# Centring each token ahead of its transposes instead of folding the mean into the first layer's weights, with a new order table, in a gated linear-attention and MLP kernel on Trainium2

## The chip, the cores and the metric

The kernel runs on one core of one Trainium2 chip. The metric is the time on the device in microseconds, from the start to the end of one execution; lower is better. The core has five engines that run their own queues in order: PE (matrix products and transposes, into PSUM), DVE (VectorE), ACT (ScalarE), POOL (GpSimd) and SP, which here only issues DMAs.

## The reference

The program first runs a gated linear recurrence for every batch (4) and head (8), over 768 steps with 48 channels, then puts the heads side by side (8 x 48 = 384) and runs a layer norm and a two-layer MLP on each token:

```python
mag = np.sqrt(a_re * a_re + a_im * a_im)
scale = np.minimum(mag, 0.999) / (mag + 1e-06)
a_re_n, a_im_n = (a_re * scale, a_im * scale)
for t in range(S):
    new_re = ar * S_re - ai * S_im
    new_im = ar * S_im + ai * S_re
    S_re, S_im = (new_re + k_t v_t^T, new_im)      # 48 x 48 for each batch and head
    y[t] = q_t @ S_re
x = y as (batch, 768, 384)
mu = mean(x); var = mean((x - mu) ** 2)
xn = (x - mu) / np.sqrt(var + 1e-06) * g_ln
out = x + np.maximum(xn @ w_ch1, 0.0) @ w_ch2      # w_ch1: 384 x 1536, w_ch2: 1536 x 384
```

The matrix products run in bf16 with sums in fp32.

## The kernel before

The recurrence is computed in chunks of 128 steps. Two chunks of one batch make a pair; there are 12 pairs P (three for each batch) and 24 chunks n = 2P + c. "Token" below means such a chunk of 128 tokens. Pair 0 has its first stage in two parts (heads 0 to 3 and 4 to 7; `PARTS`), so its steps have names such as `ks.0.1.0`.

For each pair the steps are, by their names in the table:

- loads by SP: `are`, `aim` (the gate), `k`, `q`, `vf` (k, q, v of one chunk each, 192 KB). POOL issues the loads of the two weight matrices (`wl.0` to `wl.5`), which are cast to bf16 on the way.
- decay and phase: `ln`, `iv`, `u`, `th` on ACT, `r`, `r2`, `l`, `lc` on DVE, POOL or ACT; `dec` and `ph` are sums over the steps as matmuls; `e`, `en`, `sin`, `cos` on ACT. For a pair in `QUARTER` the cosine comes from a quarter turn that two more matmuls (`qt`) add to the phase; otherwise from `abs` on ACT or DVE.
- `ke`, `qe`, `ks`, `qs`: k and q times decay and trigonometric factors, on DVE or POOL. Their transposes: `kT`, `qT` on PE followed by a copy `ksT`, `qsT` out of PSUM, or a DMA transpose issued by SP under the same name `ksT`, `qsT`.
- per chunk n: `am` (scores), `atm` (mask), `gm` and `G` (state passed on; `dps`, `decc` give its decay), `v` (cast of v), `y` (output of the recurrence, in PSUM), `x` (its copy to SBUF in bf16).
- the MLP: `bn` (mean and variance of x, on DVE), `xtr` and `xT` (x transposed on PE, copied out of PSUM), `mm1.P.g.part` (first layer, both tokens of the pair, six matmuls each), `relu`, `mm2.n.part` (second layer, four matmuls each), `rstd`, and the output: `ot` on DVE (scale by rstd and add x in one instruction from PSUM) or `oa` on ACT and `ot` on POOL; `st` stores.

The layer norm is folded: the factor 1/sqrt(var) is applied to the output of the second layer (`oa` or `ot`). The mean is taken off through the weights: `wgc` (three DVE instructions, L380) makes the matrix gc = g_ln / 384, `wp` (L389, nine matmuls of 512 columns) gives the column means of g_ln * w_ch1 in PSUM, and `wc` (L393, nine DVE instructions of 128x512) replaces w1b, the bf16 copy of w_ch1, by g_ln * w_ch1 less that mean. So x is transposed as it is, `xtr` needs `x` alone, and `bn` is wanted by `rstd` only. The first `mm1` needs all `wc` of its third of the columns.

At the start PE runs 113 filler matmuls (`warm`, L776) between the real ones.

The order is written out by hand: `PLAN` is one list of `name:engine` with the PSUM bank behind the engine's letter (P, A, V, G for POOL, S). Each engine gets its steps in the order of the list, and nothing is moved later. A step may carry `@other`: it then also waits until `other` has finished (used on POOL, "turns at the shared port"). `RINGS` gives the number of buffers of each tile; `x` has 10.

Of the kernel before, what the change touches and what calls it, by code (L numbers as in the profile page):

```python
# [56 lines left out]
ph.0.1:P1 l.2.0:V qe.0.1.0:V qe.0.0.0:V sin.0.1:A1 ph.0.0:P0 q.1.1:S k.1.0:S lc.2.0:V dps.0:P6 car.0.1:V1
dec.2.0:P2 pad.ks.1:G vf.0.0:S vf.0.1:S car.0.0:A0 qs.0.1.1:V sin.0.0:A0 qt.0.1:P1 qs.0.0.1:V qe.1.0.1:V
decc.0:V6 qt.0.0:P0 th.2.0:A aim.3.0:S cos.0.1:A1 ks.0.1.1:V ks.0.0.1:V cos.0.0:A0 ph.1.0:P4 sin.1.0:A4 k.1.1:S
tab.log.2:A ln.3.0:A ks.0.1.0:V qs.0.1.0:V en.2.0:A2 qs.0.0.0:V warm.103:P1 warm.104:P1 warm.105:P1 warm.106:P1  # L60
warm.107:P1 warm.108:P1 qT.0:P6 pad.qs.1:G ks.0.0.0:V car.1.0:V4 wl.2:G qT.1:P0 iv.3.0:A wp.1:P1 qsT.0:V6
qsT.1:V0 kT.0:P6 qs.1.0.1:G@ks.0.0.0 wc.1.1:V1 qt.1.0:P4 wc.1.0:V1 ksT.0:A6 wp.0:P0 e.2.0:A2 aim.4.0:S wc.1.2:V1
kT.1:P7 am.0:P2 tab.trig.3:A cos.1.0:A4 v.0:A wc.0.0:V0 wc.0.1:V0 wc.0.2:V0 ph.2.0:P0 ksT.1:V7 am.1:P6
ke.1.0.0:G@wc.0.2 wp.2:P4 atm.0:V2 sin.2.0:A0 gm.0:P5 G.0:A5 are.4.0:S y.0:P2 x.0:A2 qt.2.0:P0 r.3.0:G gm.1:P5
atm.1:V6 cos.2.0:A0 ke.1.0.1:V y.1:P3 x.1:A3 qs.1.0.0:V vf.1.1:S xtr.0:P2 ks.1.0.1:V vf.1.0:S ks.1.0.0:V
warm.109:P6 warm.110:P6 warm.111:P6 warm.112:P6 qT.2:P6 xT.0:A2 qT.3:P0 xtr.1:P1 qsT.2:V6 kT.3:P2 xT.1:V1
r2.3.0:G@ks.1.0.0 kT.2:P3 ksT.3:V2 mm1.0.0.0:P6 ksT.2:V3 th.3.0:A v.1:G qsT.3:A0 am.3:P0 tab.log.4:A ln.4.0:A
G.1:V5 wl.3:G mm1.0.0.1:P6 mm1.0.1.1:P2 atm.3:V0 mm1.0.1.0:P2 am.2:P0 relu.0.0:A6 q.2.1:S wc.2.2:V4 relu.0.1:A2
gm.2:P5 G.2:A5 wl.4:G wl.5:G u.3.0:A k.2.0:S ph.3.0:P6 y.3:P2 wc.2.0:V4 qe.2.0.1:G@wc.2.0 atm.2:V0 y.2:P3 x.3:A2
q.3.1:S x.2:A3 gm.3:P5 wc.2.1:V4 iv.4.0:A mm1.0.2.0:P0 xtr.2:P4 pad.ks.2:G k.2.1:S xtr.3:P3 xT.2:A4  # L70
ke.2.0.0:G@wc.2.1 abs.3.0:V6 car.3.0:V6 xT.3:V3 G.3:V5 bn.2:V mm1.0.2.1:P0 q.2.0:S tab.trig.5:A sin.3.0:A6
bn.1:V bn.3:V mm1.1.0.1:P2 mm1.1.1.1:P4 mm1.1.1.0:P4 ke.2.0.1:G cos.3.0:A mm1.1.0.0:P2 mm2.1.0:P6 mm2.0.0:P7
vf.2.0:S relu.1.1:A4 relu.1.0:A2 mm1.1.2.1:P4 are.6.0:S mm2.1.1:P6 relu.0.2:V0 r.4.0:G r2.4.0:G th.4.0:A bn.0:V
qe.2.0.0:G l.3.0:V mm2.0.1:P7 mm2.2.0:P2 tab.log.6:A u.4.0:A lc.3.0:V q.3.0:S are.5.0:S qs.2.0.0:V dec.3.0:P0
rstd.0:G e.3.0:A0 ks.2.0.1:V mm2.2.1:P2 qs.2.0.1:V en.3.0:A0 mm1.1.2.0:P4 ks.2.0.0:V mm2.1.2:P6 l.4.0:V lc.4.0:V
dps.3:P3 qe.3.0.0:G@lc.4.0 qT.4:P0 rstd.1:A qT.5:P1 relu.1.2:V4 vf.2.1:S mm2.2.2:P2 k.3.0:S dec.4.0:P4
qe.3.0.1:G ln.6.0:A oa.1:A6 qsT.4:V0 kT.4:P0 mm2.0.2:P7 qs.3.0.0:V qs.3.0.1:V k.3.1:S iv.6.0:A decc.3:V3
ln.5.0:A qT.6:P6 ksT.4:V0 mm2.3.0:P0 e.4.0:A4 dps.4:P3 v.2:G@qs.3.0.1 en.4.0:A4 ot.2:V2 ot.0:V7 ke.3.0.1:G
gm.4:P2 qsT.5:A1 ksT.5:S am.4:P4 aim.5.0:S qsT.6:V6 mm2.3.1:P0 G.4:A2 decc.4:V3 qT.7:P1 iv.5.0:A ph.4.0:P2
atm.4:V4 tab.trig.7:A sin.4.0:A2 aim.6.0:S am.5:P6 ke.3.0.0:G ks.3.0.1:G ks.3.0.0:V qsT.7:V1 k.4.1:S abs.4.0:A2  # L80
vf.3.1:S vf.3.0:S kT.6:P5 kT.7:P1 y.4:P4 q.5.0:S car.4.0:A2 r.5.0:G@ks.3.0.0 x.4:A4 r.6.0:G v.3:G mm2.3.2:P0
ot.1:G th.5.0:A atm.5:V6 y.5:P2 vf.4.0:S ksT.6:V5 xtr.4:P3 am.6:P4 vf.4.1:S k.4.0:S ksT.7:V1 am.7:P6 xT.4:V3
q.4.1:S q.4.0:S x.5:A2 xtr.5:P1 cos.4.0:A ph.5.0:P2 xT.5:A1 k.5.0:S atm.6:V4 ot.3:V0 q.5.1:S st.3:S gm.6:P1
mm1.2.1.1:P4 atm.7:V6 y.6:P0 mm1.2.1.0:P4 th.6.0:A G.6:A1 sin.5.0:A2 r2.6.0:G y.7:P6 x.6:V0 abs.5.0:A2
relu.2.1:V4 x.7:A6 gm.7:P1 xtr.6:P0 mm1.2.2.0:P2 G.7:V1 ke.4.0.1:G xtr.7:P6 xT.6:V0 r2.5.0:G mm1.2.0.1:P4
xT.7:V6 bn.6:V cos.5.0:A mm1.2.0.0:P4 ke.4.0.0:G relu.2.0:V4 st.1:S mm1.3.0.0:P6 qe.4.0.1:G tab.log.8:A u.5.0:A
u.6.0:A mm1.3.0.1:P6 mm1.2.2.1:P2 mm1.3.1.0:P4 l.5.0:V qe.4.0.0:V lc.5.0:V qs.4.0.1:V relu.3.0:A6 ks.4.0.0:V
aim.7.0:S ks.4.0.1:V mm1.3.1.1:P4 qs.4.0.0:V are.7.0:S dec.5.0:P6 mm1.3.2.0:P0 relu.2.2:A2 relu.3.1:A4 e.5.0:A6
l.6.0:V mm2.4.0:P2 are.8.0:S qT.8:P5 lc.6.0:V en.5.0:A6 aim.8.0:S ln.7.0:A iv.7.0:A bn.7:V ke.5.0.0:G@lc.6.0
mm2.5.0:P4 dec.6.0:P6 qsT.8:V5 qe.5.0.0:G kT.9:P3 bn.5:V k.5.1:S v.4:A r.7.0:G mm1.3.2.1:P0 relu.3.2:V0 ln.8.0:A  # L90
bn.4:V en.6.0:A6 ksT.8:S iv.8.0:A ksT.9:V3 mm2.6.0:P5 qe.5.0.1:G mm2.4.1:P2 mm2.6.1:P5 am.8:P0 mm2.6.2:P5
rstd.3:G mm2.5.1:P4 e.6.0:A6 qsT.9:S am.9:P6 gm.8:P3 rstd.2:A mm2.4.2:P2 r2.7.0:V u.7.0:A st.2:S tab.trig.9:A
th.7.0:A atm.8:V0 ph.6.0:P0 atm.9:V6 q.6.0:S y.8:P6 st.0:S sin.6.0:A0 ke.5.0.1:G@r2.7.0 G.8:V3 qs.5.0.0:G
vf.6.1:S y.9:P7 x.9:A7 ot.4:V2 mm2.7.0:P2 mm2.5.2:P4 are.9.0:S ks.5.0.0:V x.8:V6 ks.5.0.1:V qs.5.0.1:V
qe.6.0.0:V bn.8:V gm.9:P3 xtr.9:P7 car.6.0:A0 abs.6.0:A0 oa.5:A4 cos.6.0:A xT.9:V7 r.8.0:G@qe.6.0.0 mm2.7.1:P2
ph.7.0:P0 bn.9:V q.6.1:S qe.6.0.1:G car.7.0:A0 abs.7.0:A0 xtr.8:P7 xT.8:V7 k.6.0:S mm2.7.2:P2 G.9:V3
mm1.4.1.0:P6 oa.7:A2 sin.7.0:A0 qT.11:P4 mm1.4.1.1:P6 mm1.4.2.1:P2 qs.6.0.0:V vf.5.1:S mm1.4.0.1:P0 l.7.0:V
mm1.4.0.0:P0 relu.4.1:V6 q.7.0:S vf.5.0:S mm1.4.2.0:P2 ke.6.0.0:G@l.7.0 lc.7.0:V qsT.11:A4 qsT.10:S k.6.1:S
qs.6.0.1:V kT.11:P4 ksT.10:S tab.log.10:A ln.9.0:A st.4:S aim.10.0:S vf.6.0:S relu.4.2:A2 aim.9.0:S
ke.6.0.1:G@qs.6.0.1 relu.4.0:V0 dec.7.0:P6 v.5:V ot.6:V5 rstd.4:A ks.6.0.1:V mm2.9.0:P0 iv.9.0:A en.7.0:A6  # L100
# [712 lines left out]
```

## Time and profile before

| | us |
|---|---|
| median of 3 runs | 189.22 (188.66 to 189.74) |
| the profiled execution's own time | 187.9 |
| its span, first to last instruction | 186.1 |
| PE, DVE, ACT, POOL busy | 174.0, 157.7, 158.4, 104.6 |
| first `mm1` starts | 38.1 |
| last `mm2` ends | 182.0 |
| mean granted clock of TensorE | 0.995 of full |

The span is taken by the hardware profiler; the execution's own time has 1.8 us around it. Busy PE includes the filler matmuls (15.6 us by themselves), and matmuls overlap in the pipeline, so that the mean of one in the groups (272 ns for 256 columns) is longer than what it adds in a row (0.655 us for six, or 109 ns each).

### The profile page before, as it was taken

How to read it: one execution, taken by the hardware profiler on the slowest of the kernel's cores; microseconds unless marked ns; L12 is line 12 of the kernel's file. 1: busy time of each engine (PE TensorE's matmuls, PEld its weight loads, DVE VectorE, ACT ScalarE, POOL GpSimd, SP SyncE). 2: the span in 40 equal slices, each digit the busy share in tenths (PEclk: the TensorE clock that was granted, in tenths of full speed). 3: DMA queues.
4: the chain of work that ended last, by engine and by line, in shares of the span. 5: the costliest groups of instructions: out<-in, count | busy, mean ns of one | idle time of the engine just before them, and what ended most of it. 6: DMA issues, size and time to landing. Idle time of an engine off the chain costs nothing.

```text
span 186.1 us, 5096 instructions
## 1 busy us (share of the span) xinstructions
PE 174.0 (94%) x2012; PEld 136.2 (73%) x2012; DVE 157.7 (85%) x281; ACT 158.4 (85%) x226; POOL 104.6 (56%) x126
## 2 busy tenths in 40 slices
...
GB/s 138 281 254 216 188 237 266 171 227 180 213 154 253 221 185 284 210 206 188 206 227 225 182 251 249 212 277 151 201 224 186 210 202 225 153 232 137 36 85 129
DMA packets 132935, 37.55 MB, mean 202 GB/s; under 512 B 127152, under 2 KB 132912, under 8 KB 132912
## 3 DMA queue, kind: packets, MB, share of 16 engines
...
q8 instruction: 15, 0.25, 0.5%
...
## 4 chain that ended last, share of the span: by engine, by line
PE 81%; DVE 6%; DMA 4%; POOL 3%; SPq 2%; issue 1%; ACT 1%; POOLq 0%; DVEq 0%; ACTq 0%
PE banks L726 26%; PE banks L747 25%; PE banks L622 6%; PE banks L599 5%; PE banks L501 4%; PE banks L482 3%; PE banks L672 3%; PE banks L650 2%; PE banks L693 2%; DVE w1b L393 2%; PE banks L675 2%; DMA aim<-in_a_im_dram 2%; DMA k<-in_k_dram 2%; PE banks L497 2%; POOL ke L294 2%
## 5 line engine op out<-in xcount | busy, mean ns | idle before, releaser
L747 PE MATMUL banks<-w2b,h 128*128 128x384 bf16 x288 | 55.9, 326 | 0.0
L726 PE MATMUL banks<-xT,w1b 128*128 128x256 bf16 x432 | 51.8, 272 | 0.0
L726 PEld LDWEIGHTS <-w1b 128*128 128x128 bf16 x432 | 41.3, 98 | 6.6 <-DVE xT L291 0.7
L747 PEld LDWEIGHTS <-h 128*128 128x128 bf16 x288 | 25.7, 97 | 12.3 <-ACT h L737 0.2
L294 POOL TENSOR_TENSOR ke<-k,en 128x384 bf16<-128x384 f32 x19 | 18.4, 976 | 26.8 <-DMA k<-in_k_dram 9.6
L294 DVE TENSOR_TENSOR atm<-banks,mask 128x1024 bf16<-128x1024 f32 x24 | 29.0, 1220 | 2.0 <-PE banks L622 0.6
L781 ACT ACT_TABLE_LOAD x19 | 24.4, 1283 | 1.1 <-PEq L797 0.8
L737 ACT ACTIVATE h<-banks 128x1024 bf16<-128x1024 f32 x22 | 21.8, 1020 | 3.6 <-PE banks L726 3.5
L739 DVE TENSOR_SCALAR h<-banks 128x1024 bf16<-128x1024 f32 x14 | 17.0, 1221 | 4.7 <-PE banks L726 4.6
L759 POOL TENSOR_TENSOR ot<-ot,x 128x384 f32<-128x384 f32 x12 | 10.9, 913 | 16.5 <-ACT ot L752 11.0
L294 POOL TENSOR_TENSOR qe<-q,e 128x384 bf16<-128x384 f32 x16 | 14.5, 917 | 7.0 <-ACT en L486 3.0
L776 PE MATMUL banks<-u_e 128*128 128x256 f16 x113 | 15.6, 299 | 2.2 <-POOL one_b L320 2.2
L294 POOL TENSOR_TENSOR ks<-ke,trig 128x768 bf16<-128x768 bf16 x8 | 13.0, 1642 | 6.0 <-ACT h L737 2.1
L622 PE MATMUL banks<-qsT,ksT 128*128 128x128 bf16 x192 | 14.5, 219 | 1.1 <-ACT e L486 1.1
L776 PEld LDWEIGHTS <-u_e 128*128 128x128 f16 x113 | 12.0, 108 | 4.6 <-POOL u_e L328 1.9
L622 PEld LDWEIGHTS <-ksT 128*128 128x128 bf16 x192 | 12.4, 98 | 3.1 <-issue 0.6
L467 ACT ACTIVATE r<-r,one_b 128x768 f16<-128x768 f16 (+1 forms) x13 | 11.3, 883 | 2.7 <-DVE r L294 2.6
L289 ACT CAST x<-banks 128x384 bf16<-128x384 f32 x18 | 8.4, 481 | 5.8 <-PE banks L675 5.2
L685 DVE BATCH_NORM_STATS2 stats<-x 128x6 f32<-128x384 bf16 x24 | 13.1, 547 | 0.1
L471 DVE SCALAR_TENSOR_TENSOR l<-r,w 128x768 f16<-128x768 f16 (+1 forms) x13 | 11.9, 914 | 1.1 <-ACT r L467 1.0
L294 POOL TENSOR_TENSOR r<-aim,are 128x768 f16<-128x768 f32 x6 | 10.9, 1819 | 3.2 <-DMA q<-in_q_dram 2.6
L453 ACT ACTIVATE w<-are 128x768 f32<-128x768 f32 (+1 forms) x13 | 10.3, 793 | 1.9 <-DMA are<-in_a_re_dram 1.9
...
## 6 DMA issues: line engine op xcount, KB each, us to landing
...
```

The source lines that it names most:

```text
L294: {"DVE": nc.vector, "POOL": nc.gpsimd}[eng(name)].tensor_tensor(**kw)
L467: add(f"u.{X}", lambda S_=S_: act(out=S_("r2"), in_=S_("r2"), func=AF.Ln, bias=one_b), needs=[f"r2.{X}", "one"], uses=[("r2", P)])
L471: nc.vector.scalar_tensor_tensor(out=S_("l"), in0=S_("r2"), scalar=0.5, in1=S_("w"), op0=ALU.mult, op1=ALU.add)
L622: nc.tensor.matmul(ps[:, h], lhsT=T("ksT", n)[:, h], rhs=T("qsT", n)[:, h], start=True, stop=True)
L685: nc.vector.bn_stats(out=T("stats", n), in_=T("x", n))
L726: nc.tensor.matmul(ps[:, jj], lhsT=w1b[:, dc, ts(gi * JG + jj, C)], rhs=T("xT", P)[:, dc].rearrange("p c t -> p (c t)"), start=(dc == 0), ...
L737: act(out=dst, in_=src, func=AF.Relu)
L739: nc.vector.tensor_scalar(out=dst, in0=src, scalar1=0.0, scalar2=None, op0=ALU.max)
L747: nc.tensor.matmul(bank(f"o.{n}")[:, 0:DM], lhsT=T("h", P)[:, j, ts(c, C)], rhs=w2b[:, j], start=(j == 0), stop=(j == NJ - 1))
L759: nc.gpsimd.tensor_tensor(out=T("ot", n), in0=T("ot", n), in1=T("x", n), op=ALU.add)
L776: g.add(f"warm.{i}", lambda i=i: nc.tensor.matmul(bank(f"warm.{i}")[:, 0:256], lhsT=u_e[:, 0, 0], rhs=u_e[:, 1].rearrange("p j t -> p (j t ...
L781: g.add(f"tab.{nm}.{i}", lambda tab=tab: nc.scalar.preload_act_table_set(tab))
```

## The change

Every token is now centred by itself. A new step `xc` (128x384, bf16 in and out, DVE or POOL) subtracts the mean that `bn` has found, a tile ring `xc` of four buffers holds the result, and `xtr` transposes `xc` in place of `x`. So the order for a token is x, bn, xc, xtr, xT, mm1. The residual still takes x. The weights are only scaled: nine steps `ws` (128x512, on ACT or POOL) multiply w1b by g_ln; `cmean`, `gc`, `wgc`, `wp` and `wc` are gone. Pair 3 is added to `QUARTER`, and there are 118 filler matmuls.

```diff
-         ... "x": 10, "stats": 4,
+         ... "x": 10, "xc": 4, "stats": 4,
-QUARTER = {0, 1, 2}
+QUARTER = {0, 1, 2, 3}
...
-    def wgc():
-        ...
-                nc.vector.tensor_scalar(out=gc[:, dc], in0=cmean, scalar1=gln[:, ds(dc, 1)],
-                                        scalar2=None, op0=ALU.mult)
     for jb in range(NG):
-        o = f"wp.{jb}"
-        def wp(jb=jb, o=o):
-            for dc in range(ND):
-                nc.tensor.matmul(bank(o), lhsT=gc[:, dc], rhs=w1b[:, dc, ts(jb, 512)], ...)
-        g.add(o, wp, needs=["wgc", f"wl.{jb}"], ps=(o, 1))
         for ec in range(ND):
-            g.add(f"wc.{jb}.{ec}", lambda ...: nc.vector.scalar_tensor_tensor(
-                out=w1b[:, ec, ts(jb, 512)], in0=w1b[:, ec, ts(jb, 512)], scalar=gln[:, ds(ec, 1)],
-                in1=bank(o), op0=ALU.mult, op1=ALU.subtract), needs=[o], ps=(o, 1))
+            def ws(jb=jb, ec=ec):
+                piece = w1b[:, ec, ts(jb, 512)]
+                if eng(f"ws.{jb}.{ec}") == "ACT":
+                    nc.scalar.mul(out=piece, in_=piece, mul=gln[:, ds(ec, 1)])
+                else:
+                    {"DVE": nc.vector, "POOL": nc.gpsimd}[eng(f"ws.{jb}.{ec}")].tensor_scalar(
+                        out=piece, in0=piece, scalar1=gln[:, ds(ec, 1)], scalar2=None, op0=ALU.mult)
+            g.add(f"ws.{jb}.{ec}", ws, needs=["gln", f"wl.{jb}"])
...
+            def f_xc(n, c):
+                mean = T("mv", P)[:, c, 0:1]
+                {"DVE": nc.vector, "POOL": nc.gpsimd}[eng(f"xc.{n}")].tensor_scalar(
+                    out=T("xc", n), in0=T("x", n), scalar1=mean, scalar2=None, op0=ALU.subtract)
+            add(f"xc.{n}", lambda n=n, c=c: f_xc(n, c), needs=[f"bn.{n}"],
+                uses=[("x", n), ("mv", P), ("xc", n)])
             def f_xtr(n):
                 ...
-                    nc.tensor.transpose(ps[:, dc], T("x", n)[:, ts(dc, C)], ident)
+                    nc.tensor.transpose(ps[:, dc], T("xc", n)[:, ts(dc, C)], ident)
...
-    for i in range(113):
+    for i in range(118):
```

The order table is a new one from its first entry to its last. Counted over the whole table, these steps have moved to other engines (V is DVE, A is ACT, G is POOL, S a DMA):

| step | before | after |
|---|---|---|
| abs | V 3, A 6 | V 1, A 7 |
| atm | V 24 | V 22, two as A copy (`ac`) and G mask |
| car | V 5, A 4 | V 4, A 5 |
| ke | G 19, V 5 | G 15, V 9 |
| qe | G 16, V 8 | G 19, V 5 |
| ks | V 18, G 8 | V 19, G 7 |
| ksT | A 1, V 9, S 14 | V 11, S 13 |
| qsT | V 10, A 3, S 11 | V 11, A 2, S 11 |
| ot | V 12, G 12 (with 12 `oa` on A) | V 17, G 7 (with 7 `oa` on A) |
| r | V 7, G 6 | V 6, G 7 |
| r2 | V 7, G 4, A 2 | V 7, G 2, A 4 |
| rstd | G 5, A 7 | G 9, A 3 |
| v | A 4, G 6, V 2 | A 4, G 7, V 1 |
| x | A 18, V 6 | A 14, V 10 |
| xT | A 7, V 17 | A 8, V 16 |
| xc | | V 15, G 9 |
| ws | | G 5, A 4 |

The stretch of the new table up to the first `mm1`, from the first cosine on:

```
qt.0.0:P0 qt.0.1:P3 th.2.0:A k.1.0:S decc.1:V2 cos.0.0:A0 cos.0.1:A3 qe.0.0.0:G@qe.0.1.0 decc.0:V5
ks.0.0.1:V v.0:V ph.1.0:P6 q.1.1:S aim.3.0:S lc.2.0:V ks.0.1.1:V qs.0.0.1:V sin.1.0:A6 vf.1.1:S ks.0.0.0:V
dec.2.0:P0 ks.0.1.0:V tab.log.2:A e.2.0:A0 qs.0.1.1:V wl.2:G qs.0.1.0:V pad.qs.1:G wl.1:G kT.1:P3 car.1.0:V6
gm.0:P2 qs.0.0.0:V warm.103:P4 warm.104:P4 warm.105:P4 qT.1:P5 ke.1.0.0:G@qs.0.0.0 en.2.0:A0 kT.0:P4 ksT.1:V3
qT.0:P3 ln.3.0:A qsT.1:V5 am.1:P0 qe.1.0.1:G G.0:A2 warm.106:P5 warm.107:P5 warm.108:P5 gm.1:P2 ksT.0:V4
qt.1.0:P6 iv.3.0:A ks.1.0.1:G qsT.0:V3 am.0:P4 ws.0.1:G atm.1:V0 y.1:P3 ph.2.0:P0 qs.1.0.1:G G.1:V2 atm.0:V4
tab.trig.3:A cos.1.0:A6 qs.1.0.0:V y.0:P2 x.1:A3 sin.2.0:A0 warm.109:P4 qT.3:P3 bn.1:V x.0:A2 qT.2:P4 qsT.3:A3
ks.1.0.0:G@qs.1.0.0 ws.2.2:A bn.0:V qsT.2:V4 are.4.0:S warm.110:P2 warm.111:P2 warm.112:P2 warm.113:P2
warm.114:P2 kT.3:P2 aim.4.0:S ws.0.2:G xc.0:V xc.1:V r.3.0:G@xc.1 kT.2:P3 ws.0.0:A ws.1.0:G xtr.0:P4 ksT.3:V2
ws.1.2:G vf.1.0:S xtr.1:P5 xT.1:V5 qt.2.0:P0 xT.0:V4 ws.1.1:A am.3:P6 ws.2.0:A cos.2.0:A0 mm1.0.0.0:P4 ksT.2:V3
```

More of the change, by code (lines that the diff above doesn't have):

```diff
@@ L57 @@
[L57 to L100, printed above, removed]
-ks.6.0.0:G@ks.6.0.1 ksT.11:V4 gm.10:P1 q.7.1:S mm2.9.1:P0 am.10:P2 mm2.9.2:P0 ot.5:G am.11:P4 G.10:V1 e.7.0:A6
@@ L142 @@
[L142 to L145 removed]
+are.0.0:S ue:G uth:V are.0.1:S tab.log.0:A ln.0.1:A iv.0.1:A one:G ln.0.0:A iv.0.0:A aim.0.0:S r.0.0:V
```

182 lines of the change are left out of this document (104 added, 78 removed), and 2 rows, old and new, of the table RINGS.

## The prediction

> **What bounds the kernel now.** I read the page's busy time first, then the windows (columns: window; length, then busy us and instructions of each engine, granted clock, DMA share, GB/s), then the chain in order of time (start us, us, what).
>
> ```profile
> PE 174.0 (94%) x2012; PEld 136.2 (73%) x2012; DVE 157.7 (85%) x281; ACT 158.4 (85%) x226; POOL 104.6 (56%) x126
> ```
>
> ```profile
> 24.00:30.00 6.00, 4.69 (x49) 3.29 (x48) 5.91 (x15) 5.97 (x9) 1.86 (x2) 1.00 1.20 258
> 30.00:36.00 6.00, 4.64 (x73) 3.46 (x73) 6.00 (x9) 5.61 (x9) 2.69 (x2) 1.00 0.97 205
> 36.00:42.00 6.00, 6.00 (x88) 5.64 (x87) 5.78 (x10) 5.97 (x8) 4.53 (x5) 1.00 1.05 216
> 156.00:162.00 6.00, 6.00 (x88) 4.57 (x86) 4.98 (x7) 2.43 (x3) 3.80 (x4) 1.00 1.01 194
> ```
>
> ```profile
> 26.05 0.56 DVE car L514
> ...
> 27.85 4.04 DVE w1b L393 x6
> 31.93 0.32 PE banks L497
> ...
> 38.24 0.66 PE banks L726 x6
> ...
> 178.08 3.91 PE banks L747 x24
> 182.02 0.62 DVE ot L761
> ```
>
> Two stages. From 36 us to 182 PE never pauses: the chain there is PE alone. Ahead of that DVE is full (5.91 and 6.00 of 6) and PE is not, and the chain runs through DVE, with 4.04 us in six corrections of w1b (L393). So the time is: when PE becomes full, plus PE's own work, plus a tail of 4.1 us (182.0 to 186.1). The first matmul of the first layer (mm1.0.0.0) starts at 38.08 in the timeline. What must be asked of the change: does it bring that forward, does it alter PE's work behind it, and does it open holes there.
>
> **Prices.** Groups with shapes kept apart (busy us, mean ns | idle before):
>
> ```profile
> L393 DVE SCALAR_TENSOR_TENSOR w1b<-w1b,gln,banks 128x512 bf16<-128x512 bf16 x9 | 6.2, 739 | 0.0
> L685 DVE BATCH_NORM_STATS2 stats<-x 128x6 f32<-128x384 bf16 x24 | 13.1, 547 | 0.1
> L474 DVE TENSOR_SCALAR l<-l 128x384 f16<-128x384 f16 x2 | 0.5, 259 | 0.1
> L761 DVE SCALAR_TENSOR_TENSOR ot<-banks,rstd,x 128x384 f32<-128x384 f32 x12 | 7.2, 609 | 2.6 <-PE banks L747 2.6
> L361 POOL MEMSET ks<- 128x512 bf16 x3 | 1.6, 524 | 0.1
> ```
>
> - xc on DVE (15): nearest is L474, same size and width, 0.26; with a scalar per row at most L761's 0.61. I take 0.31, nearer to L474 because all its data is 16 bits wide in SBUF.
> - xc on POOL (9): a 128x768 cast there takes 0.84 (L419), a memset of 512 elements 0.52. I take 0.60, bounds 0.4 and 0.84.
> - ws on POOL (5): the same two rows, I take 0.65. ws on ACT (4): its copy of 384 elements takes 0.48, of 1024 1.03; so 0.6.
>
> **PE's work, part by part.** Removed: wp, three times three matmuls, 0.65 us each (chain: L389 x3), so 1.95, all ahead of 38 us where PE waits anyway: worth nothing directly. Behind the first mm1: am.3 (0.45, L622 x8) now stands ahead of it; one more quarter turn (qt.3) adds 0.33, one more kT (its ksT was a DMA transpose) 0.45, and three of the warm-ups (0.12 each) now lie behind it: 143.9 (182.0 - 38.1) - 0.45 + 0.33 + 0.45 + 0.35 = 144.6 us.
>
> **DVE, ACT and POOL in total.** DVE: corrections -6.2 and gc -0.7; xc +4.7 (15 x 0.31); the regrouping of ot, x, ke, ksT (+), qe, r, abs, atm (-) by their rows +1.0: -1.2. ACT: seven oa instead of twelve (-2.9), fewer x and rstd, plus two ac (2 x 1.0) and ws 2.4: about -1.3. POOL: xc 5.4 and ws 3.2 are new; with rstd and qe up, ke, ot, ks and r2 down, +7. No engine but PE gets near full by this.
>
> **When PE becomes full.** I walk the new order with the rows' durations. DVE, queue order: the value cast v.0 now stands on DVE (it was on ACT) and holds the queue until vf.0.0 lands. That load is SP's 18th; 4.3 MB up to and with it and a part of w1b have to move, and the GB/s row has moved 4.1 MB by 18.6 us and 5.0 by 23.3: 21.0 to 21.5. Then v.0, lc.2, seven ks and qs halves (0.3 each) and car.1: qs.0.0.0 ends at 24.4 to 24.9 (25.75 before). Four copies ksT/qsT (0.6 each; one of them was on ACT), atm.1 (1.15), G.1 (0.5), atm.0 (1.15): 29.6 to 30.1. Before, the six corrections stood between, and the second atm ended at 34.77. So five us are won here, and part is given back at once: the first mm1 now needs x, bn and xc of both tokens. ACT gives x.0 at 31.0 (it stands behind a table load of 1.28 and sin.2). DVE: qs.1.0.0, bn.1 and bn.0 (0.66 each, were at 46 to 50 us), qsT.2, xc.0, xc.1: 33.0. POOL's ks.1.0.0 (1.64, which kT.3 waits for) ends at 32.1 to 32.7, and its ws.0.2 then meets xc.0: up to 0.65 more. ksT.3 (0.6), xT.1, xT.0 (0.3 each): mm1.0.0.0 starts between 34.5 and 35.5, I take 35.0. The scaling itself lies on POOL and ACT beside this and is done at 33.4. POOL is next in line: behind xc.1 it has r.3 (1.8), ws.1.0, ws.1.2, then v.1, ready at 37.0 to 37.9; PE wants it for gm.2 2.8 us behind the first mm1, at 37.8. Cover there is nil; ws at 0.84 would cost 0.5.
>
> **Behind it: holes?** Each token now has x, bn, xc between y and xtr. I add up the PE work that the table puts between y.n and xtr.n, against x 0.5, bn 0.73, xc, and 0.3 of hand-overs (from y.0's end to x.0 it was 0.21). Before, 0.82 to 3.7 us lay there for x alone, least slack 0.14, and no hole shows. After, 1.9 to 4.3 (token 4: 7.1): token 20 has gm.21, dps.10, mm2.18.1, mm2.19.2 and xtr.21, 0.2 + 0.2 + 0.65 + 0.65 + 0.17 = 1.87 against 1.82. Least slack with xc on DVE: 0.05, 0.10 and 0.30 (tokens 20, 3, 23); on POOL 0.44 to 0.98 (and 4.9 at token 4). So xc is hidden by mm2, ph and dec; at 0.61 on DVE it would cost 0.25 + 0.2 = 0.45 at tokens 20 and 3.
>
> Loads: gln and k.0.0 stand one place later in SP's queue behind k.1.1 (0.8 us of transfer), in the walk above. Later loads were issued 4.5 us or more ahead of use (q.10 at 136.8 for 141.3), the landing row says 4.2; I take the same lead.
>
> **Sum.** 35.0 + 144.6 = 179.6 against 182.0; tail 4.1 as before (last mm2, one ot of 0.62, one store): span 183.7, 2.4 less. The profiled run took 187.9 for its 186.1, so 185.5 here; the median 189.2 lies 1.3 above the profiled one, so 186.8. A measurement of this kernel can tell about 0.5% (0.95 us) from no change.
>
> **Rivals.**
> 1. *The start is not shortened so far.* ACT (5.97 of 6 at 24 to 30) or POOL takes DVE's place: with vf.0.0 landing 1 us late, ws at 0.84 and xc at 0.61, mm1 starts 1.0 + 0.5 + 0.3 later, and 0.45 is lost at tokens 20 and 3: +2.2, 189.0; half of that, 187.9. For it: POOL has no cover at gm.2. Against: each needs the end of its bounds. Chance 0.18.
> 2. *Slower: xc on POOL comes late.* Eight of the nine tokens there (not token 4) have 0.44 to 0.98 slack, mean 0.63. POOL works in order and shares with DVE: if xc waits for one ks of 1.64 in front of it, each token loses 1.0, 8 us in all, 194.9. It becomes a loss from (2.4 + 0.95) / 8 = 0.42 a token; midway 191. For it: in the timeline a DVE r<-r took 1.16 us against 0.55 elsewhere while POOL ran a ke, and that ke 1.41 against 0.91. Against: behind 36 us only five DVE instructions are stretched, by 0.14 to 0.39, and POOL is idle 44%. Chance 0.17. The Trainium skill (SBUF — State Buffer, "SBUF: two separate sides") calls the pair of ports that VectorE and GpSimd share an exclusive lock: whoever is first keeps it for its whole instruction and the other is blocked. The stretched pair at 15 us agrees with this; by that rule an xc on DVE that starts just behind a POOL ks would take up to 1.64 more; at a mean of 0.8 over the 15 on DVE, less their slack, the sum would come out at 191 to 195, as in this rival.
> 3. *Loads come late.* With PE 2 to 3 us earlier and DMA share near 1.0 all along, a k or q lands behind its use: +3, 189.8. Against: past the start the table of waits names one wait for a DMA over 2 us (POOL's r, 2.6, at 89.5). Chance 0.05.
>
> **How the numbers follow.** Forecast 0.60, from 185.0 (start 34.5, without the 0.8 by which the 143.9 exceed its matmuls at the chain's rates, 143.1, and 0.5 of spread of the runs) to 188.2. Rival 1 is half faster, half same. Faster 0.60 + 0.09 = 0.69; same 0.09 + 0.04 (rival 3 and weak forms of 2) = 0.13; slower 0.18. The range 185.0 to 190.8 leaves out some 0.05 below and the stronger half of rival 2 above, 0.1.
>
> **What would show it.** Right: no L393 rows, mm1's first matmul near 35, windows of PE at 6.00 from 36 on, last matmul near 179.6, xc near 0.31 on DVE and 0.60 on POOL. Wrong: PE idle behind 38 us with xc or xT as releaser (rival 2), v or w1b from POOL as releaser at 34 to 40 (rival 1), DMA as releaser (rival 3).

## The result, and the profile after

| | before | after |
|---|---|---|
| median of 4 runs each, us | 189.24 (188.66 to 189.74) | 198.1 (197.66 to 199.3) |
| the profiled execution's own time and span, us | 187.9, 186.1 | 199.3, 197.6 |
| first `mm1` starts, last `mm2` ends, us | 38.08, 181.98 | 38.84, 193.78 |

The changed kernel takes 1.048 times as long (95% interval 1.0423 to 1.0536): 8.9 us slower, where 2.4 us faster was forecast. Ratios here and below are of undisturbed runs of both kernels on the same chip, so they are not always the quotient of the medians. The profiled execution of after is the longest of its four; the other spans are 196.0 to 196.7.

The page first: busy time, and the shares of the chain in before and in after.

```profile
PE 81%; DVE 6%; DMA 4%; POOL 3%; SPq 2%; issue 1%; ACT 1%; POOLq 0%; DVEq 0%; ACTq 0%
```

```profile
PE 179.1 (91%) x2018; PEld 137.6 (70%) x2018; DVE 158.5 (80%) x290; ACT 158.9 (80%) x218; POOL 123.1 (62%) x142
...
PE 38%; DVE 19%; POOL 13%; DMA 11%; SPq 6%; issue 6%; ACT 4%; POOLq 0%; DVEq 0%; ACTq 0%
```

POOL went up by 18.5 us and carries 13% of the chain instead of 3%; PE carries 38% instead of 81%. The windows of after (window; length, then busy us and instructions of PE, PEld, DVE, ACT and POOL, granted clock, DMA share, GB/s):

```profile
24.00:30.00 6.00, 4.75 (x48) 3.92 (x49) 5.01 (x13) 4.73 (x7) 2.06 (x3) 0.72 1.23 232
30.00:36.00 6.00, 4.86 (x80) 3.71 (x78) 5.97 (x9) 3.59 (x6) 5.50 (x4) 1.00 1.02 236
36.00:42.00 6.00, 5.11 (x62) 3.79 (x59) 5.97 (x12) 5.84 (x8) 6.00 (x5) 1.00 1.08 211
42.00:48.00 6.00, 4.88 (x66) 3.86 (x67) 2.05 (x4) 3.37 (x6) 5.96 (x6) 0.72 0.99 236
72.00:78.00 6.00, 5.08 (x83) 3.89 (x81) 4.43 (x10) 4.75 (x7) 6.00 (x6) 1.00 0.05 17
```

From 36 us on PE was to be full. It is not, and where it is shortest (36 to 48, 72 to 78) POOL shows 6.00 or 5.96 of 6: POOL is the full engine there. In other short windows it is not (60 to 66: PE 5.25, POOL 4.26; 114 to 126: PE 5.33 and 5.47, POOL 3.80 and 3.64); there one late step stops PE, as the waits below show. The chain in order of time (start us, us, what) has POOL alone from 35 to 52 us but for short gaps of issue:

```profile
17.72 6.56 DMA vf<-in_v_dram
...
24.37 0.56 DVE v L407
...
35.01 1.64 POOL ks L296
36.65 1.07 POOL w1b L381
...
38.15 1.83 POOL r L296
39.98 3.08 POOL w1b L381 x2
43.06 0.80 POOL v L407
...
47.65 1.28 POOL xc L680
```

Why POOL is full stands in the groups, shapes kept apart (busy us, mean ns of one | idle before): L680 is xc, L381 and L379 are ws on POOL and on ACT.

```profile
L680 POOL TENSOR_SCALAR xc<-x,mv 128x384 bf16<-128x384 bf16 x9 | 11.3, 1253 | 8.3 <-DVE mv L674 8.3
L381 POOL TENSOR_SCALAR w1b<-w1b,gln 128x512 bf16<-128x512 bf16 x5 | 7.8, 1571 | 0.0
L680 DVE TENSOR_SCALAR xc<-x,mv 128x384 bf16<-128x384 bf16 x15 | 4.9, 339 | 0.4
L379 ACT ACTIVATE w1b<-w1b,gln 128x512 bf16<-128x512 bf16 x4 | 2.6, 712 | 0.0
```

An xc on POOL takes 1.25 us where 0.60 was taken, a ws 1.57 where 0.65 was. Who waits for them is in the table of waits (engine and line <- releaser: us in total, times, longest):

```profile
PEld L688 <- POOL xc L680: 5.5, 7, 1.3
PEld L721 <- POOL w1b L381: 2.5, 2, 1.4
```

PEld is PE's loading of a matmul's weights, L688 is `xtr`, L721 is `mm1`. Followed along PE's queue from the start of one matmul to the start of the next, less the first one's work (some 0.16 more than the idle time that the profile shows), PE pauses behind the first `mm1` in mm1.0.1.1, ahead of its first matmul (0.99) and from its third on (1.71, of which 1.3 are the wait and 0.4 the half-speed matmuls that follow), both for ws; at mm2.1.1 and mm2.0.2 (0.40 and 0.91) for w2b, whose loads POOL issued late; and at xtr.5, 6, 10, 12, 13, 16 and 18 (1.04, 0.28, 0.86, 0.68, 0.40, 0.57, 0.62), all for an xc on POOL: 2.7 + 1.3 + 4.45 = 8.5 us. In the DMA queue's own waits SP stands 12.8 us behind POOL's `ot` with two stores (longest 6.7), which is the window at 72 with a DMA share of 0.05: loads behind those stores in SP's queue wait too.

### The profile page after: what moved, and what is told of

Same layout as the page of the kernel before. It is cut to its first block, busy times and chain, and to the rows that moved or that the text cites. A ratio compares the mean times of both kernels' runs of the same rounds, so it can differ in the third digit from the quotient of the medians.

```text
span 197.6 us, 5126 instructions
## 1 busy us (share of the span) xinstructions
PE 179.1 (91%) x2018; PEld 137.6 (70%) x2018; DVE 158.5 (80%) x290; ACT 158.9 (80%) x218; POOL 123.1 (62%) x142
## 4 chain that ended last, share of the span: by engine, by line
PE 38%; DVE 19%; POOL 13%; DMA 11%; SPq 6%; issue 6%; ACT 4%; POOLq 0%; DVEq 0%; ACTq 0%
PE banks L721 13%; PE banks L742 13%; POOL xc L680 6%; DMA vf<-in_v_dram 5%; DMA w2b<-in_moe_w_ch_dram 4%; SPq L397 4%; DVE atm L296 4%; POOL w1b L381 3%; PE banks L610 3%; DVE ks L296 2%; DVE stats L673 2%; POOL r L296 2%; DVE l L459 2%; SPq L438 2%; PE banks L688 2%
## 5 line engine op out<-in xcount | busy, mean ns | idle before, releaser
L721 PE MATMUL banks<-xT,w1b 128*128 128x256 bf16 x432 | 52.9, 275 | 2.0 <-POOL w1b L381 2.0
L721 PEld LDWEIGHTS <-w1b 128*128 128x128 bf16 x432 | 41.1, 98 | 8.6 <-POOL w1b L381 2.5
L296 DVE TENSOR_TENSOR atm<-banks,mask 128x1024 bf16<-128x1024 f32 x22 | 26.5, 1216 | 1.9 <-PE banks L610 1.7
L296 POOL TENSOR_TENSOR ke<-k,en 128x384 bf16<-128x384 f32 x15 | 14.0, 934 | 20.6 <-DVE l L459 9.8
L296 POOL TENSOR_TENSOR qe<-q,e 128x384 bf16<-128x384 f32 x19 | 17.8, 938 | 8.0 <-DVE l L462 3.4
L771 PE MATMUL banks<-u_e 128*128 128x256 f16 x118 | 17.0, 299 | 2.2 <-POOL one_b L320 2.2
L680 POOL TENSOR_SCALAR xc<-x,mv 128x384 bf16<-128x384 bf16 x9 | 11.3, 1253 | 8.3 <-DVE mv L674 8.3
L296 POOL TENSOR_TENSOR r<-aim,are 128x768 f16<-128x768 f32 x7 | 12.7, 1818 | 2.7 <-ACT en L474 1.6
L756 DVE SCALAR_TENSOR_TENSOR ot<-banks,rstd,x 128x384 f32<-128x384 f32 x17 | 10.0, 612 | 4.1 <-issue 2.9
L754 POOL TENSOR_TENSOR ot<-ot,x 128x384 f32<-128x384 f32 x7 | 6.3, 913 | 11.0 <-ACT xT L291 8.5
L470 PE MATMUL banks<-l,u_e 128*128 128x384 f16 (+1 forms) x52 | 9.8, 313 | 3.6 <-DVE l L462 3.6
L660 PE MATMUL banks<-v,atm 128*128 128x48 bf16 x192 | 12.5, 185 | 0.4 <-DVE atm L296 0.3
```

Source lines behind the costliest of these rows:

```text
L296: {"DVE": nc.vector, "POOL": nc.gpsimd}[eng(name)].tensor_tensor(**kw)
L660: nc.tensor.matmul(ps[:, h], lhsT=T("atm", n)[:, h], rhs=T("v", P)[:, c, h], start=True, stop=nfirst)
L680: {"DVE": nc.vector, "POOL": nc.gpsimd}[eng(f"xc.{n}")].tensor_scalar(out=T("xc", n), in0=T("x", n), scalar1=mean, scalar2=None, op0=ALU.s ...
L721: nc.tensor.matmul(ps[:, jj], lhsT=w1b[:, dc, ts(gi * JG + jj, C)], rhs=T("xT", P)[:, dc].rearrange("p c t -> p (c t)"), start=(dc == 0), ...
L771: g.add(f"warm.{i}", lambda i=i: nc.tensor.matmul(bank(f"warm.{i}")[:, 0:256], lhsT=u_e[:, 0, 0], rhs=u_e[:, 1].rearrange("p j t -> p (j t ...
```

## The experiments

The theory: what POOL's two new instructions cost is the cause. A first rival, of the table: the regrouped order leaves too little room for x, bn and xc whichever engine has them. A second, of the start: nothing is won there, since something else binds next. The expectations name their theories with letters of their own and say what each means; their times in us are to be read against the forecast's kernel before, at 188 to 190. Each edit is to the changed kernel unless said otherwise.

| kernel | ratio to before | 95% interval |
|---|---|---|
| ws_on_act | 1.0327 | 1.0252 to 1.0402 |
| xc_on_dve | 1.0407 | 1.0327 to 1.0488 |
| both_off_pool | 1.032 | 1.025 to 1.0391 |
| pool_imm | 1.0334 | 1.0235 to 1.0433 |
| pool_two_ops | 1.0434 | 1.0346 to 1.0523 |
| tuned | 1.029 | 1.0178 to 1.0401 |
| before_scaled | 0.9976 | 0.9923 to 1.003 |
| before_centred | 1.198 | 1.1889 to 1.2072 |
| ws_mult_add | 1.0192 | 1.0162 to 1.0222 |
| xc_mult_add | 1.0285 | 1.0165 to 1.0405 |
| fast_form | 0.9985 | 0.9942 to 1.0028 |
| fast_form_v0 | 0.991 | 0.9869 to 0.9951 |
| fast_form_v0_warm | 0.9986 | 0.9956 to 1.0015 |

**Off POOL, one at a time and both.**

```diff
 # ws_on_act (both_off_pool has this and the next)
-ws.0.1:G ws.0.2:G ws.1.0:G ws.1.2:G ws.2.1:G
+ws.0.1:A ws.0.2:A ws.1.0:A ws.1.2:A ws.2.1:A
 # xc_on_dve, at tokens 2, 4, 5, 6, 10, 12, 13, 16, 18
-xc.2:G ... xc.13:G@lc.8.0 ...
+xc.2:V ... xc.13:V ...
```

> The changed kernel, with the five ws that are on POOL put on ACT at the same places of the table. Theory P (price): a POOL instruction with a scalar per row takes 1.57 us at 128x512 and 1.25 at 128x384 where 0.65 and 0.60 were taken for it; what is lost behind it is lost to that. Then the two pauses of PE in front of mm1.0.1.1 and behind it (1.0 and 1.7) go, qs.1 and v.1 on POOL come earlier, and w2b is asked for earlier: 192 to 194.5 us. Rival L (length): x, bn, xc in a row are too long for the work that covers them, on whatever engine: at most 1 us better, 197. Rival V (the load of v for pair 0 and the half clock behind its wait): this lies ahead of the ws and stays, 197.

Measured 1.0327 (194.45 us, the slow end of theory P). The first `mm1` starts at 35.23, where the forecast had it (35.0); here v.0's load was also in time (21.34, against 24.37 in after). ACT's queue is no free place, though: it does seven ws in a row (33.04 to 37.44), and mm1.0.1.1 waits 1.20 for the PSUM bank that cos.2.0, behind them, still reads; y.3 waits 1.44 for G.2, later in the same queue. All pauses for xc stay (xtr.5 1.03, xtr.10 0.85, and so on).

> The changed kernel, with the nine xc that are on POOL put on DVE at the same places of the table. Theory P: PE's pauses in front of xtr.5, 6, 10, 12, 13, 16 and 18 (4.5 us added up) go and xc takes 0.3: 192.5 to 194.5 us. Rival L: DVE is as full as before, so xc comes as late there: 197 or more. Rival V: 197.

Measured 1.0407 (196.07 us, short of theory P's 194.5). The two pauses for ws stay (0.99 and 1.33). DVE pays in other places: xtr.13 waits 1.40, xtr.17 0.81, and the mean of its xc rises from 339 to 419 ns.

> Both moves together: five ws on ACT, nine xc on DVE, the rest of the table as it was. Theory P: all that POOL's price cost goes, and what is left against the forecast of 186.8 is the late v of pair 0 (3 us): 188 to 190.5. Rival L: 195 or more. Rival V alone: 196.

Measured 1.032 (194.44 us), though POOL has neither step: theory P's 188 to 190.5 was missed. The first `mm1` is at 35.12, and PE waits for ACT and DVE instead (mm1.0.1.1 1.20, y.3 1.44, xtr.13 1.41, xtr.17 0.80), and at mm2.0.2 1.06 for w2b. The two pauses at `xtr` have a cause of their own. Timeline of both_off_pool (start us, us, instruction):

```profile
119.49 1.80 POOL L296 TENSOR_TENSOR r<-aim,are 128x768 f16<-128x768 f32 x1 [3.54 <-DVE l L462]
119.87 1.54 DVE L680 TENSOR_SCALAR xc<-x,mv 128x384 bf16<-128x384 bf16 x1
```

xc.13 starts while POOL works on r.10 and ends at 121.41, 0.12 behind it: 1.54 us where the median xc takes 0.32. xc.16 ends 0.11 behind a qe of POOL (0.95 us), xc.4 0.12 behind an r (0.53). So an xc on DVE can still be held up by POOL. Here the rival of the table looked as good as the theory: to move the load is not the same as to take the price away, so these three runs could not tell the two apart.

**Is it the per-row scalar?** Constants in its place, on POOL alone.

```diff
-scalar1=gln[:, ds(ec, 1)]        # ws on POOL
+scalar1=1.0
-scalar1=mean                     # xc on POOL
+scalar1=0.0
```

> The changed kernel with its table as it was, but the five ws and nine xc on POOL take a constant (times 1.0, minus 0.0) in place of a scalar per row; so nine tokens are not centred and five ninths of the weights not scaled. Theory P in its strict form (it is the scalar per row that costs): 128x384 takes 0.5 to 0.7 us, 128x512 0.6 to 0.85, and the time falls to 188 to 190.5. If it is POOL's bf16 tensor_scalar itself that is slow, or the shared port: 1.25 and 1.57 again, and 198.

```profile
L681 POOL TENSOR_SCALAR xc<-x 128x384 bf16<-128x384 bf16 x9 | 10.6, 1180 | 5.5 <-ACT x L291 3.4 <-DVE x L293 1.4 <-DVE l L462 0.6
L381 POOL TENSOR_SCALAR w1b<-w1b 128x512 bf16<-128x512 bf16 x5 | 7.4, 1491 | 0.0
```

Only 0.07 to 0.08 us less each: the scalar's kind is not the cause. Here xc doesn't wait for bn's mean either, and v.0's load was in time (21.80), so the ratio (1.0334) holds other differences too.

**Is it the lone operation?** The kernel's own cast `v` on POOL, 0.83 us for 768 elements, is a multiply with an add behind it. A second operation, add 0.0, put behind both:

```diff
-scalar1=gln[:, ds(ec, 1)], scalar2=None, op0=ALU.mult)
+scalar1=gln[:, ds(ec, 1)], scalar2=0.0, op0=ALU.mult, op1=ALU.add)
-scalar1=mean, scalar2=None, op0=ALU.subtract)
+scalar1=mean, scalar2=0.0, op0=ALU.subtract, op1=ALU.add)
```

> The changed kernel, its table as it was, with xc and ws on POOL written with a second operation (plus 0.0) behind the first. The cast v on POOL has two operations and takes 0.83 us for twice the elements of xc, which takes 1.25 with one operation and 1.18 with a constant. Theory P2 (it is the form with one operation that is slow): xc 0.45 to 0.7, ws 0.5 to 0.8, PE's pauses in front of xtr go, 190 to 192 us. Rival (16-bit input or the output's rounding is slow on POOL, whatever the form): 1.2 and 1.5 again and 197 to 198.

```profile
L682 POOL TENSOR_SCALAR xc<-x,mv 128x384 bf16<-128x384 bf16 x9 | 14.2, 1583 | 7.9 <-DVE mv L675 7.8
L381 POOL TENSOR_SCALAR w1b<-w1b,gln 128x512 bf16<-128x512 bf16 x5 | 3.5, 701 | 0.0
```

The two went apart. Multiply-add brought ws from 1.57 to 0.70; subtract-add brought xc from 1.25 to 1.58. With them went the pauses: those of ws are gone, those of xc grew (xtr.5 1.70, xtr.10 1.20, xtr.12 1.02). The ratio, 1.0434, is that of after within the noise.

**The start and the table by themselves.** Before's table with `wp` and `wgc` left out and `wc` turned into a scaling on DVE; then the same with bn and xc on DVE right behind every x; and the new table with xc on DVE right behind bn and ws in ACT's gaps and on DVE.

```diff
 # before_scaled, in before's table
-wgc:... wp.0:... wc.0.0:V... 
+ws.0.0:V ...
 # before_centred, on top of it
-x.0:A2 ... bn.0:V
+x.0:A2 bn.0:V xc.0:V ...
 # tuned, in the new table
-ws.0.1:G ws.0.2:G ws.1.0:G ws.1.2:G ws.2.0:A ws.2.1:G ws.2.2:A
+ws.0.1:A ws.0.2:A ws.1.0:A ws.1.2:A ws.2.0:V ws.2.1:V ws.2.2:V
```

> The kernel before, with its own table, from which wgc, wp and the memset for them are taken out and whose nine wc on DVE only scale; no token is centred, so the subtraction of the mean is left out altogether. It prices what the change can win. Theory F (DVE sets when PE becomes full): six scalings of 0.35 in place of corrections of 0.74, and gc's 0.7 gone: the first mm1 comes 2 to 3 us earlier and the time falls by as much, 185.5 to 186.5 where the kernel before has 188.3. Rival (ACT's copies, POOL or the loads end next): less than 1 us, 187.5 to 188.3.

Measured 0.9976, no change that can be told. With 3.6 us less of w1b's work on DVE (9 x 739 ns became 9 x 344) PE waits for something else: in its profile (an execution of 191.5 us) am.0 stands idle for 2.50 us until ACT is through with the copy ksT.0 and with e.2.0 behind it, whose PSUM bank am.0 takes. In before the same wait is there with 1.12. So the rival of the start holds for the old table; that the gain comes with the regrouping, which took that copy off ACT, fits the first `mm1` at 35 us in the runs on the new table, but no run moves that copy alone.

> The kernel before, with its own table: the corrections replaced by scalings on DVE as in the run beside it, bn moved right behind x, and xc on DVE right behind bn; all else stands where it stood. It is the centring without the new table. Theory L (length): the PE work between y and xtr is 0.8 to 3.7 us there and x, bn, xc and hand-overs need 1.8; the shortage adds up to 13 us over the 24 tokens, part of it shared by the two tokens of a pair: 194 to 199 us. Rival: the two-deep work of PE hides it and DVE's saved 2 to 3 us show: 186 to 189.

```profile
PEld L696 <- DVE xc L688: 17.2, 15, 2.0
```

Measured 1.198. Centring put into a table that was not made for it costs some 37 us. 17.2 of them are PE waiting at `xtr` for xc on DVE, at 15 places; others come behind (atm, dec and the output stand in DVE's queue too). The expectation, 199 at most, was far too low. So the place of bn and xc in the table matters far more than their own time.

> The changed kernel with nothing of the change on POOL: every xc on DVE right behind its bn; ws.0 and two of ws.1 on ACT in the pauses that ACT had between 31 and 36 us, ws.2 on DVE behind atm.2. Theory P and a rest from the places in the table: the pauses at xtr.13 (1.4), gm.3 (1.4) and mm1.0.1.1 (1.2) of the run with both moved shrink: 190.5 to 192.5. Theory L: the rest of the pauses stays, 194.

Measured 1.029 (195.15 us; 190.5 to 192.5 was hoped for). One attempt at giving POOL's load to the others by hand gained no more than the plain moves. The mean of xc on DVE rose to 499 ns, its longest to 1.66 us, beside an r of POOL.

**The price taken away, the table kept.** ws alone as multiply-add; xc alone, on POOL and DVE, as -x + mean (multiply by -1, then add), with -g_ln for the weights so that the signs cancel; and both. A small step `ngl` on DVE (3 numbers a row) makes -g_ln.

```diff
 # ws_mult_add
-scalar1=gln[:, ds(ec, 1)], scalar2=None, op0=ALU.mult)
+scalar1=gln[:, ds(ec, 1)], scalar2=0.0, op0=ALU.mult, op1=ALU.add)
 # xc_mult_add (with mul=ngl for the weights)
-scalar1=mean, scalar2=None, op0=ALU.subtract)
+scalar1=-1.0, scalar2=mean, op0=ALU.mult, op1=ALU.add)
 # fast_form: both, ws with ngl
```

> The changed kernel with its table as it was; ws on POOL is written as times g, plus 0.0. The run with two operations showed 0.70 us for that form where the single multiplication takes 1.57, and 1.58 for subtract-then-add at xc. So this is the ws price alone, with nothing moved to another engine. Theory P: the first mm1 at 35 to 36, v.1 4 us earlier than in the changed kernel, no pause in front of mm1.0.1.1: 193.5 to 195 where the kernel before has 188 to 190 (3 to 4 less than the changed kernel). Theory L: at most 1 less.

> The changed kernel with xc alone as x times -1 plus mean (multiply-add); ws stays one multiply, by -g_ln. Theory P (each form costs what its pauses showed, and the two add up): xc 0.59 on POOL, no pause ahead of xtr.5, 10, 12, 13, 16 and 18 (4.2 us in the changed kernel), but the two pauses for ws at the first mm1 stay (2.7 us and half a clock behind them): ratio 1.02 to 1.03. Rival (POOL's queue is the matter, and with ws slow xc comes late all the same): xtr pauses of over 2 us stay, ratio 1.035 or more. Second rival (ws is hidden and xc is the whole loss): ratio below 1.01.

> The changed kernel with its table as it was, all xc written as x times -1 plus mean, all ws as times -g (a 128x3 negation of g on DVE is added), so that both have the multiply-add form on POOL; the two signs cancel in the first layer. Theory P (the price on POOL is the whole cause): xc on POOL 0.5 to 0.7 and ws 0.7, no pause of over 0.3 us in front of an xtr: ratio to the kernel before 0.985 to 0.995, as the forecast had it. Rival L (the longer path x, bn, xc, xtr and the table's own places): pauses stay on DVE's tokens, ratio 1.01 to 1.025.

The groups of xc and ws on POOL in fast_form:

```profile
L692 POOL TENSOR_SCALAR xc<-x,mv 128x384 bf16<-128x384 bf16 x9 | 5.3, 589 | 8.3 <-DVE mv L686 7.5 <-DVE l L474 0.4 <-DMA q<-in_q_dram 0.4
L392 POOL TENSOR_SCALAR w1b<-w1b,ngl 128x512 bf16<-128x512 bf16 x5 | 3.4, 693 | 0.0
```

Neither form: 1.048. ws alone: 1.0192, 2.9 points less. xc alone: 1.0285, 2.0 less. Both: 0.9985, 5.0 less; the median of all 12 runs of fast_form is 191.75 us beside 191.12 for before on the same chip. So with both forms the loss is gone with no step moved but the small ngl added, and the rival of the table has no share in the loss that could be told. That is the theory; the 0.985 to 0.995 that it expected was not quite reached. That the two shares add up so well is in part luck. In xc_mult_add no pause for xc at tokens 5 to 18 is above 0.28 any more, but qT.3 waits 4.7 us for POOL's qs.1.0.1 and the first `mm1` comes at 41.59. Of that ws.0.1 ahead of it (1.88 us) explains some 1.2; more comes from loads, since POOL's ke waits 3.04 us for k and its qe 3.15 for q. And of the 10.2 us between the profiles of after and fast_form (197.6 and 187.4) some 2.2 belong to the load of v.0, which came late in after: with ws alone mended and the load as late, the first `mm1` is at 38.13 (35 to 36 was expected), in fast_form at 35.90.

**What is left at the start.** v.0 moved on DVE from ahead of lc.2 to behind car.1; and 12 more fillers.

```diff
 # fast_form_v0
-ks.0.0.1:V v.0:V ph.1.0:P6 ... car.1.0:V6 gm.0:P2
+ks.0.0.1:V ph.1.0:P6 ... car.1.0:V6 v.0:V gm.0:P2
 # fast_form_v0_warm, on top of it
-ph.1.0:P6 
+ph.1.0:P6 warm.118:P2 ... warm.129:P2
```

> The same, and the cast v.0 on DVE moved behind the ks, qs and car that stood behind it, so that the queue does not wait for the load of v. Theory V: 0.5 to 2.6 us of DVE's wait at 22 us come off the first mm1, time 0.5 to 2 lower than without. Rival: gm.0 on PE and G.0 on ACT wait for v.0 instead: within 0.5.

> The same once more, with twelve filler matmuls between ph.1.0 and dec.2.0. Theory K (the granted clock): in the profiles of the changed kernel it fell to 0.72 of full at 24 to 30 us and at 42 to 48, after PE had idled 2.5 us; the fillers keep PE busy there, the clock stays at 1.00 and the spread between runs of one kernel shrinks, median 0.5 to 1 lower. Rival: the fillers stand in front of dec.2.0 and cost up to 1.4.

fast_form_v0 is at 0.991 (0.9869 to 0.9951): 0.9% faster than before. The fillers bring it back to 0.9986, 0.8 points more. In the profile of fast_form_v0 the granted clock was 1.00 in every window from 18 to 48 us, so in that run they had nothing to save; their cost is what the rival said. Windows of fast_form_v0, to be held against those of after at 36, 42 and 72 us (xc.5 starts at 73.15 in after and at 64.74 here, so the last one is taken 8.4 us earlier):

```profile
36.00:42.00 6.00, 5.68 (x89) 4.53 (x87) 5.08 (x9) 5.95 (x9) 5.48 (x7) 1.00 0.97 174
42.00:48.00 6.00, 6.00 (x60) 5.08 (x58) 6.00 (x12) 5.94 (x8) 3.89 (x5) 1.00 1.17 185
63.60:69.60 6.00, 6.00 (x93) 4.99 (x92) 5.38 (x14) 5.95 (x9) 5.71 (x7) 1.00 1.04 204
```

In that stretch POOL is still near full (5.71 of 6), but PE is full and the DMA share is 1.04 in place of 0.05. SP's wait for POOL's `ot` fell from 12.8 us to 6.3, so the long stop of the loads was POOL's doing too.

**The forms by themselves.** 24 tensor_scalar instructions of 128x384 into bf16 at the end of POOL's queue, every form twice in a row.

```diff
+for i, f in enumerate(FORMS):      # (elements, source, scalar1, op0, scalar2, op1)
+    g.add(f"probe.{i}", lambda i=i, f=f: probe(i, f), ...)
```

> The changed kernel with 24 more POOL instructions and 4 more DVE instructions behind its last store, when no other engine works: tensor_scalar of 128x384 into bf16, each form twice on POOL (multiply; subtract; add; multiply by a constant; multiply-add; multiply-subtract; multiply-multiply; add-multiply; subtract-multiply; add-add; and multiply and multiply-add with fp32 in). The whole time is of no interest, only the mean of one. Theory P1 (only multiply followed by add has a fast way on POOL, everything else is slow): multiply-add 0.55 to 0.60, all other single operations 1.2 to 1.3, all other pairs 1.5 to 1.7. Theory P2 (the subtraction and the lone operation are the trouble, pairs without a subtraction are fast): multiply-multiply, add-multiply and add-add near 0.6 too, multiply-subtract and subtract-multiply 1.5 or more. Theory P3 (a neighbour on the shared ports stretched the instructions, the form has little to do with it): single multiply and subtract fall to 0.6 to 0.8 here, where nothing runs beside them. On DVE all four forms between 0.25 and 0.4.

They began at 183 us, so the first few ran beside the last output steps; all from 193.6 on ran alone, and so did the first add (188.44, 1.25 us; DVE idle until 190.41, ACT done at 188.13). One window holds two instructions of a form (window; length, POOL busy us and instructions, granted clock, DMA share, GB/s). In this order: subtract; multiply by a constant; multiply-add; multiply-subtract; add-multiply; add-add; multiply from fp32; multiply-add from fp32.

```profile
185.72:188.40 2.68, 2.49 (x2) 1.00 0.17 59
...
191.08:193.62 2.54, 2.34 (x2) 0.94 0.44 158
193.62:195.15 1.53, 1.31 (x2) 0.50 0.00 0
195.15:198.62 3.47, 3.30 (x2) 0.50 0.00 0
...
200.15:201.68 1.53, 1.32 (x2) 0.50 0.00 0
...
205.17:208.66 3.49, 3.30 (x2) 0.50 0.00 0
208.66:211.36 2.70, 2.48 (x2) 0.50 0.00 0
211.36:212.82 1.46, 1.31 (x2) 0.50 0.00 0
```

So one operation takes 1.24 to 1.26 (1.17 with a constant) whether it multiplies, subtracts or adds, and whatever the input's type. Multiply-add, multiply-multiply and add-multiply take 0.66. Add-add and every pair with a subtraction take 1.65. None of the three theories had this whole: P1 was wrong on two fast pairs, P2 on add-add, and P3 (a neighbour stretches them) falls, since the slow ones are as slow alone (the add, the multiply from fp32, the slow pairs). DVE's four took 0.32 to 0.38. The Trainium skill (Perfetto Trace Analysis, "GPSIMD Engine Instruction") warns against reported spans on this engine and asks for the spacing of starts: the spacing here is 1.34 against 0.76, each 0.1 over its span, so the ranking is the same.

## Why the prediction was wrong, step by step

The row of before that the first point turns on:

```profile
L294 POOL TENSOR_TENSOR ke<-k,en 128x384 bf16<-128x384 f32 x19 | 18.4, 976 | 26.8 <-DMA k<-in_k_dram 9.6
```

- **The step that failed: "xc on POOL ... I take 0.60, bounds 0.4 and 0.84" and "ws on POOL (5): the same two rows, I take 0.65".** Measured 1.253 and 1.571, both beyond the bound. The bound came from the cast L419, by size alone. That cast is a multiply-add in the code, xc is a lone subtract and ws a lone multiply, and no row of before shows POOL doing either at such a size (its one lone operation there, the add in rstd, has 128x2). The row to bound from was the slowest per element of POOL's large rows, ke: 0.976 us for the very 128x384 of xc. Even that is short of 1.25, but it would have eaten 0.38 of the least cover of 0.44. POOL's total, "+7", was +18.5. With the form that the cast has, xc took 0.589 and ws 0.693: the prices taken were right for an instruction that the kernel didn't issue.
- **"Least slack ... on POOL 0.44 to 0.98".** Too large. With xc 0.65 over its price, 0.65 less the slack would pause PE by 0.2 at most; measured up to 1.04. The sums took xc alone and left out what stands in POOL's queue ahead of it: xc.5 starts at the end of an r that waited for xc.4, also on POOL and also 0.65 longer; xc.10 at the end of a qe, xc.13 at the end of xc.12. At tokens 12, 16 and 18 POOL stood idle until bn's mean came, and pauses of 0.57 to 0.68 for 0.65 more leave a slack of 0.1 or less, so x or bn came later than in the sums; which of the two stays open. At 0.589 the pauses are 0.20 at token 10, 0.12 at token 13 and 0.02 or less at the other seven, so the order holds, but with next to nothing to spare.
- **"ws at 0.84 would cost 0.5", "cover there is nil" at gm.2.** Right as to the place, wrong as to the size: with mm1 at 38.84 instead of 35.0 ahead of it, v.1, due at 37.0 to 37.9, ended at 43.86, and gm.2 started at 44.58. In fast_form v.1 ended at 38.76 and gm.2 started at 38.79.
- **When PE becomes full, 35.0.** The walk was right where its inputs were: 35.23 in ws_on_act, 35.12 in both_off_pool, 35.17 in fast_form_v0; 35.9 in fast_form. In after it was 38.84. The larger part is v.0, which waited on DVE for its load until 24.37; ws has a share too (v.0 in time but ws slow on POOL: 36.84 in xc_on_dve, 36.72 in pool_imm; v.0 late but ws fast: 38.13 in ws_mult_add). "21.0 to 21.5" is one of two outcomes: ahead of the other steps of DVE as it is, v.0 began at 21.3 to 21.9 in ws_on_act, xc_on_dve, both_off_pool, pool_imm, xc_mult_add and fast_form, at 24.0 to 24.5 in after, pool_two_ops, tuned and ws_mult_add. Why the load lands at either time was not settled, and a difference of a point or so between two of these runs can be this alone. In after PE idled 2.6 us for it at dec.2.0, and the granted clock of the window at 24 is 0.72. A step that holds a queue until a load lands carries that load's whole spread; moved, v.0 began at 24.19 and the first `mm1` stayed at 35.17.
- **"PE's work" 144.6.** The named work is right (kT, qt, fillers: fast_form's rows show the same prices), but PE "never pauses" was too clean: first `mm1` to last `mm2` took 147.2 in fast_form_v0. Most of the 2.6 us are pauses of 0.1 to 0.5, at mm1.0.2.1 (0.49, relu.0.1 held its bank until 41.51), gm.10 (0.40), mm1.8.1.1 (0.36), y.4 (0.32), xtr.14 (0.26) and others.
- **Right:** the two stages; xc on DVE 0.31 (0.339); the end 3.8 behind the last `mm2` (4.1); ws on ACT a little low (0.6, measured 0.712).
- **The rivals.** Rival 2 named the mechanism, xc on POOL late by more than 0.42 a token: 4.45 us over its eight tokens is 0.56. It put that down to waiting behind a ks and to the shared port; it was the instruction's own price. By the Trainium skill's rule (SBUF — State Buffer, "SBUF: two separate sides") xc on DVE could be held up by a POOL instruction that started first: in after its median was 320 ns and its longest 660, and pool_forms shows the slow forms with DVE idle, so the lock isn't what made 198. Where xc was moved to DVE the rows do look like that rule (xc.13 above, 1.54 us), but in after an xc of 0.31 ran wholly inside a ws of POOL (37.35, ws from 36.62 to 38.19). Rival 1's place (POOL at gm.2) added 2.7 us, and its late vf.0.0 came too: 2.9 us behind the 21.5 in after, where it counted with 1. Rival 3's late loads came only as w2b, issued late by POOL (1.3 us).

Sum, after against the forecast's span of 183.7: the first `mm1` 38.84 for 35.0 (+3.8), the work behind it 154.9 for 144.6 (+10.3), the tail 3.8 for 4.1 (-0.3): 197.6 with the digits kept, the measured span. Of the 10.3, 8.5 are the pauses counted above. With POOL's price as forecast (fast_form) the kernel would have come out at 0.9985 x 189.24 = 189.0, inside the range, but equal to before rather than faster. What fast_form's profile has above the forecast's span (187.4 for 183.7) is a first `mm1` 0.9 later and 3.1 us more behind it, for the most part the small pauses; v.0 didn't wait for its load in it (21.91).
